# A chunked recurrence and two MoE stages: full-height closing products, an order that knows TensorE's columns, decay products on GpSimd, and an inverse that starts from two transposes

## The chip, the cores and the metric

The kernel runs on one core of a Trainium2 chip. The metric is the device time of one execution in microseconds (us). Before the change three runs took 1219.82, 1231.59 and 1233.6 us, a median of 1231.59. The trace comes from a further execution of 1221.59 us, whose span is 1219.8 us and whose mean granted TensorE clock is 0.944 of full speed.

Engines have short names in the rows: PE is TensorE's matmul and PEld its weight load, DVE is VectorE, ACT is ScalarE, POOL is GpSimd, and SP is the engine whose queue issues most DMAs.

## The reference

```python
# recurrence, for each of B*H = 4*8 heads, S = 768 steps, D = 40
y[:, :, t] = einsum('bhd,bhde->bhe', r_t, state)
Sa = einsum('bhde,bhe->bhd', state, a_t)
state = state * w_t[:, :, None, :] - einsum('bhd,bhe->bhde', Sa, b_t) \
        + einsum('bhd,bhe->bhde', v_t, k_t)
# first MoE, on x = y as 3072 tokens x 320 (d_ff 1024)
x = ((x @ w1) * (x @ w2)) @ w3 @ w_out
# second MoE (d_ff 2048)
h = x @ w_in
out = (h * cos(h)) @ w_out2
```

## The kernel before, in words

**The recurrence** is cut into 24 chunks of 32 steps (`C`, `NC`). The 32 heads are 16 pairs; in a pair one head has partitions 0 to 39 and the other 64 to 103 (`OD`, `EV`). For each chunk `prep` (L516) runs two scans of the decay, multiplies `a` by the decay `Dt` for each parity (the two products called GA, 40x512 on VectorE), and sends GA by DMA into a ring of 7 slots (`NB`; rows name the slots r_67 to r_79). `gstage` (L546) multiplies the scaled keys by GA on TensorE, and ScalarE copies the results into `lam`, a stack of 32x32 triangular matrices, and into the ring; GpSimd masks a triangle there.

Four chunks (`GC`) form a group. Their 512 triangular matrices are inverted together: `tinv_start` (L575) transposes `lam` into `Lt` in 32 pieces of 128x32 on VectorE, `tinv` (L591) solves diagonal blocks, the middle and the corner (matrices 0 to 11 of each partition on VectorE, 12 to 15 on GpSimd, side by side), and `tfin` (L660) transposes the result in one 128x1024 step into `TT`, from which TensorE reads. `lam`, `Lt`, the work tile and `TT` exist once, so the inverse of a group starts only when the one before is read out. Then each chunk goes through `mv`, `st_z`, `st_q`, `st_u`, `st_y`, `st_s`: small products on TensorE with copies by ScalarE, masks on X by GpSimd, and products on VectorE that write the next state. `st_y` (L739) has 16 products for each half of the pairs; its results for one parity lie in columns 64 to 103 of TensorE's array, for the other in 0 to 39. The output goes to DRAM (`yd`).

**The MoE stages.** After every two chunks a slab of 256 tokens is complete. `split_x` (L866) splits it into a rounded part `xh` and a remainder; `ab` (L874) computes a piece of `x @ w1` and `x @ w2` by sums of eight products of 128x256, the eighth of which has only 64 rows (`R[H0]` times `xr`). Products of the two are stored (`pd`). Beside it w3 and w_out are folded into one matrix, and weights are converted from 64-bit floats on VectorE (`conv`: three instructions a piece, tiles `f`, `w`, `r`). When the last slab is done the second phase runs, with the second MoE, which the change leaves as it is.

**What sets the order.** Nothing is issued while the functions above run: each call is recorded (`Program`, `Queue`), `link` finds what depends on what, and `emit` (L256) plans the order with a table of costs: an instruction starts when its engine is free and its inputs are there by the table, and of several that could start the one with the longest planned path to the end goes first (`far`). Instructions are then issued in the order of their planned starts, all from line 318, so every row says L318. On the chip each engine takes its instructions in that order, and a DMA queue too; an instruction that waits holds up those behind it.

Of the kernel before, what the change touches and what calls it, by code (L numbers as in the profile page):

```python
# [4 lines left out]

# [21 lines left out]
T2 = 256  # L27
# [102 lines left out]
class Program:  # L130

    STEP, DEEP = {True: 1.67, False: 0.457}, {True: 180, False: 185}
    COST = {
        ("scalar", "copy"): (205, 0.72), ("scalar", "activation"): (200, 0.9), ("vector", "tensor_tensor"): (155, 1.1),
        ("vector", "tensor_scalar"): (80, 1.3), ("vector", "scalar_tensor_tensor"): (80, 1.6),
        ("vector", "tensor_tensor_scan"): (80, 2.3), ("vector", "transpose"): (35, 1.8),
        ("vector", "tensor_reduce"): (147, 1.04), ("vector", "memset"): (60, 0.83),
        ("gpsimd", "tensor_tensor"): (330, 2.05), ("gpsimd", "affine_select"): (250, 1.2), ("gpsimd", "memset"): (110, 0.82),  # L140
    }
# [114 lines left out]
    def emit(self, tc, nc):  # L256
        self.link()
        N = len(self.calls)
        eng = [c[0] for c in self.calls]
        cost = [self.length(n) for n in range(N)]  # L260
        after = [[] for _ in range(N)]
        for n, d in enumerate(self.deps):
            for j in d:
                after[j].append(n)
        far = [0.0] * N
        hop = lambda n, m: self.HOP[eng[n]] if eng[m] != eng[n] else self.OWN[eng[n]]
        for n in reversed(range(N)):
            x = cost[n][1] + (self.ISSUE + self.BEGIN + self.END if eng[n] == "sync" else 0)
            far[n] = x + max([far[m] + hop(n, m) for m in after[n]], default=0)
# [6 lines left out]
        lanes, moved = deque([0.0] * self.LANES), 0.0  # L276
        for n in range(N):
            if not left[n]:
                heapq.heappush(later[eng[n]], (0.0, n))
        for k in range(N):  # L280
# [4 lines left out]
            n = heapq.heappop(ready[e])[1]  # L285
            if e == "tensor":
                if more is not None and not left[more] and self.mode(n) != mode and when[more] <= t + self.WAIT:
                    if n != more:
                        heapq.heappush(ready[e], (-far[n], n))
                        n = more  # L290
                        ready[e].remove((-far[n], n)) if (-far[n], n) in ready[e] else later[e].remove((when[n], n))
                        heapq.heapify(ready[e])
                        heapq.heapify(later[e])
                        t = max(t, when[n])
                more = self.sums.get(n)
            step, whole = cost[n]
            _, method, args, kw = self.calls[n]
            if method == "matmul":
                if self.mode(n) != mode:
                    t += self.SWITCH  # L300
                mode = self.mode(n)
            if method == "dma_start":
                t = max(t, lanes.popleft())
                moved = max(moved, t + step + self.BEGIN) + whole
                whole = moved + self.END + self.STORE * (kw["out"].space == DRAM) - t
                lanes.append(t + whole)
                step += self.GAP
            start[n] = (t, k)
            free[e], end = t + step, t + whole
            for m in after[n]:  # L310
                when[m] = max(when[m], end + hop(n, m))
                left[m] -= 1
                if not left[m]:
                    heapq.heappush(later[eng[m]], (when[m], m))
        with tc.manual_schedule():
            for n in sorted(range(N), key=lambda n: start[n]):
                e, method, args, kw = self.calls[n]
                getattr(getattr(nc, e), method)(*args, **kw)  # L318


class Kernel:
# [194 lines left out]
    def prep(self, c, alt=0):  # L516
# [70 lines left out]
    def quads(t, row, col, *dims):  # L587
# [277 lines left out]

    def split_x(self, xf):  # L866
        nc = self.nc
        xh, xl, xr = self.xh, self.xl, self.xr
# [3 lines left out]
        return xh, xl, xr  # L872

    def ab(self, s, x, f):  # L874

        nc = self.nc
        xh, xl, xr = x
# [134 lines left out]
    def weights_a(self):  # L1012

        self.ks = [self.fixed[t] for t in ("k1", "k2")]
        self.xf = self.place("mid", 128, 3, T2)
        t = lambda p, *f: self.place("xs", p, *f, dt=F32R)
        self.xh, self.xl, self.xr = t(128, 3, T2), t(128, 2, T2), t(64, T2)
        self.turns["p"] = deque(self.place("mid", 128, T2) for _ in range(PB))

    def turn(self, tag):  # L1020
# [305 lines left out]
```

## Time and profile before

| what | value |
|---|---|
| median of three runs | 1231.59 us (1219.82 to 1233.6) |
| profiled execution | 1221.59 us, span 1219.8 us |
| TensorE matmul (PE) busy | 1052.4 us, 86% of the span, 13536 instructions |
| VectorE (DVE) busy | 842.2 us, 69%, 1776 instructions |
| ScalarE (ACT) busy | 679.3 us, 56%, 1750 instructions |
| GpSimd (POOL) busy | 600.4 us, 49%, 734 instructions |

These shares are averages over stages with different limits. The span begins with an opening of 52.5 us; then six times an inverse of a group alternates with a stretch of chunks without one, until the last chunks and slabs end near 703 us; then comes a passage into the second phase, which starts near 808 us and lasts to the end. In the first 148 us the granted TensorE clock is low (0.67 to 0.69 from 52.5 on), later 0.89 to 1.00.

### The profile page before, as it was taken

The numbers are of one execution on the slowest core, as the hardware profiler recorded it, in microseconds if no ns is written. First come the engines' busy times: TensorE is split into PE (matmuls) and PEld (weight loads), VectorE is DVE, ScalarE is ACT, GpSimd is POOL, SyncE is SP. The second block draws the span as 40 slices with busy tenths as digits, with TensorE's granted clock in tenths as the row PEclk, the third lists the DMA queues.
The fourth block names the chain that finished last, engine by engine and source line by source line (L and its number), as shares of the span: only waits on it lengthen the run. The fifth ranks groups of instructions, "written<-read, shape, count | busy, mean of one in ns | idle before, by whom it ended". The sixth has DMA issues, their size and how long they took to land. (4 is left out here: it accounts for less than half of the span.)

```text
span 1219.8 us, 34120 instructions
## 1 busy us (share of the span) xinstructions
PE 1052.4 (86%) x13536; PEld 956.4 (78%) x13536; DVE 842.2 (69%) x1776; ACT 679.3 (56%) x1750; POOL 600.4 (49%) x734
## 2 busy tenths in 40 slices
PE   2434798869987998999889977999999999999997
PEld 1324687768776877878778865899999999999997
DVE  9797779668968887896796674785455554545444
ACT  5865545754676578478545542455455544555443
POOL 8666336435444533563566673463455443454222
PEclk9975799889988999999899987999999999999999
DMA  6643544443454445444446553411101111011000
GB/s 177 185 117 93 140 119 123 126 137 115 129 157 131 114 141 158 127 134 114 137 136 209 150 169 106 124 39 47 46 12 46 44 38 46 22 37 46 9 4 23
DMA packets 142128, 122.73 MB, mean 101 GB/s; under 512 B 68240, under 2 KB 114832, under 8 KB 140432
## 3 DMA queue, kind: packets, MB, share of 16 engines
q1 hardware_dynamic: 141824, 120.50, 34.4%
q8 instruction: 106, 1.74, 0.6%
q14 instruction: 54, 0.44, 0.1%
q10 hardware_dynamic: 144, 0.06, 0.0%
HBM read 86.95 MB, written 29.62 MB: 96 GB/s over the span
## 5 line engine op out<-in xcount | busy, mean ns | idle before, releaser
L318 PE MATMUL bank<-xs,w 128*128 128x256 f32 (+1 forms) x1536 | 281.3, 316 | 29.9 <-ACT xs L318 22.0
L318 PEld LDWEIGHTS bank<-xs,w 128*128 128x128 f32 (+1 forms) x1536 | 221.3, 200 | 75.2 <-ACT xs L318 23.8
L318 POOL TENSOR_TENSOR w<-w,w 128x512 fp32r<-128x512 f32 x96 | 127.9, 1333 | 237.5 <-ACT w L318 147.4
L318 POOL TENSOR_SCALAR_AFFINE_SELECT X<-X 32x256 f32<-32x256 f32 (+1 forms) x144 | 98.6, 685 | 113.2 <-ACT X L318 92.1
L318 ACT COPY mid<-bank 128x256 f32<-128x256 f32 (+2 forms) x190 | 71.7, 394 | 144.9 <-PE bank L318 138.3
L318 ACT COPY X<-bank 32x128 f32<-32x128 f32 (+1 forms) x384 | 124.3, 324 | 41.8 <-PE bank L318 36.3
L318 DVE SCALAR_TENSOR_TENSOR w<-w,bank 128x512 f32<-128x512 int32 x96 | 65.8, 687 | 117.6 <-ACT w L318 106.0
L318 ACT COPY r<-bank 64x160 f32<-64x160 f32 (+2 forms) x408 | 113.4, 281 | 43.7 <-PE bank L318 38.7
L318 PE MATMUL bank<-X,r 104*40 104x72 f32 (+3 forms) x3072 | 124.2, 238 | 12.8 <-POOL X L318 7.1
L318 DVE TENSOR_TENSOR X<-bank,mid 40x128 f32<-40x128 f32 (+1 forms) x276 | 97.9, 355 | 51.0 <-PE bank L318 46.0
L318 PE MATMUL bank<-xs,r 128*128 128x256 f32 x576 | 130.5, 282 | 0.5 <-DVE xs L318 0.5
L318 PE MATMUL bank<-D,r 128*128 128x256 f32 x576 | 129.2, 282 | 1.8 <-DVE w L318 1.7
L318 PEld LDWEIGHTS bank<-X,r 104*40 104x40 f32 (+3 forms) x3072 | 104.5, 118 | 25.1 <-POOL X L318 8.6
L318 ACT CAST w<-w 128x512 fp32r<-128x512 f32 x120 | 73.6, 620 | 85.5 <-PE bank L318 70.5
L318 PE MATMUL bank<-mid 32*32 32x72 f32 (+2 forms) x3040 | 92.6, 233 | 26.6 <-ACT r L318 18.6
L318 PE MATMUL bank<-r,w 128*128 128x320 f32 x432 | 107.7, 311 | 0.6 <-ACT r L318 0.6
L318 PEld LDWEIGHTS bank<-mid 32*32 32x32 f32 (+2 forms) x3040 | 72.2, 126 | 42.7 <-ACT r L318 20.3
L318 PEld LDWEIGHTS bank<-D,r 128*128 128x128 f32 x576 | 99.2, 189 | 2.5 <-DVE w L318 2.2
L318 PEld LDWEIGHTS bank<-xs,r 128*128 128x128 f32 x576 | 99.9, 189 | 0.7 <-DVE xs L318 0.7
L318 DVE TENSOR_TENSOR sh<-sh,sh 128x110 f32<-128x110 f32 (+6 forms) x216 | 85.1, 394 | 2.4
L318 DVE SCALAR_TENSOR_TENSOR w<-w 128x512 f32<-128x512 int32 x96 | 84.6, 882 | 1.9
L318 PE MATMUL bank<-more,w 128*128 128x320 f32 x360 | 84.9, 310 | 0.0
(92 smaller groups left out, 2278.9 us busy)
## 6 DMA issues: line engine op xcount, KB each, us to landing
pd<-mid SPq DMA_DIRECT2D x96, 128.0 KB
f<-w3t SPq DMA_DIRECT2D x32, 256.0 KB
sh<-kb SPq DMA_DIRECT2D x48, 160.0 KB
sh<-wa SPq DMA_DIRECT2D x96, 80.0 KB
X<-pd SPq DMA_DIRECT2D x6, 1024.0 KB
w<-pd SPq DMA_DIRECT2D x6, 1024.0 KB
w34d<-f SPq DMA_DIRECT2D x32, 160.0 KB
r<-wo SPq DMA_DIRECT2D x16, 320.0 KB
```

Of the source, the lines that this page charges most:

```text
L318: getattr(getattr(nc, e), method)(*args, **kw)
```

## The change

The eighth product of each sum in `ab` becomes a full 128-row one: the remainder `xl` has all three parts of x, and `xr` is gone. `split_x` needs one subtraction of 128x768 for it instead of two. The two GA products of each `prep` go from VectorE to GpSimd. `tinv_start` transposes `lam` in two instructions of sixteen 128x32 pieces each. In `emit`, the costs change; a matmul is planned as holding those of four 32-column quarters of the array that its result needs (`columns`, `array`), a change of kind (up to 32 rows, up to 64 rows, more; and the number type) waits until all quarters are free, and `beside` takes a ready product of the same kind whose quarters are free ahead of one whose quarters are not. `RUNS` is 0, so the random variations are not used. The plan being another, every engine's order changes.

```diff
@@ costs @@
-    STEP, DEEP = {True: 1.67, False: 0.457}, {True: 180, False: 185}
+    STEP, DEEP = {True: 1.67, False: 0.457}, 185
-        ... ("vector", "tensor_tensor"): (155, 1.1),
+        ... ("vector", "tensor_tensor"): (165, 1.25),
-        ("gpsimd", "tensor_tensor"): (330, 2.05), ...
+        ("gpsimd", "tensor_tensor"): (380, 2.3), ...
-    HOP = {"tensor": 95, "scalar": 65, "vector": 70, "gpsimd": 40, "sync": 60}
-    ISSUE, GAP, BEGIN, RATE, END, STORE, LANES, SWITCH, WAIT = 350, 55, 1350, 380, 1100, 600, 8, 120, 100
+    HOP = {"tensor": 140, "scalar": 110, "vector": 120, "gpsimd": 90, "sync": 60}
+    ISSUE, GAP, BEGIN, RATE, END, STORE, LANES, SWITCH, WAIT = 370, 60, 1350, 380, 1600, 600, 8, 90, 100
+    RUNS, LATE, VARY = 0, 500, {"vector": (0.9, 1.25), "gpsimd": (0.9, 1.4), "scalar": (0.95, 1.1)}
@@ length @@
-            a = kw["rhs"]
-            w = min(x for x in (32, 64, 128) if x >= size(kw["lhsT"]))
-            step = 4 + self.STEP[a.dtype == F32] * size(a) * w / 128
-            return step, self.DEEP[a.dtype == F32] + step * 128 / w / 2 if a.dtype == F32 else self.DEEP[False] + step
+            f = kw["rhs"].dtype == F32
+            step = 2 + self.STEP[f] * size(kw["rhs"])
+            return step, self.DEEP + step / (2 if f else 1)
@@ mode, columns, beside @@
-        return kw["lhsT"].ap[0][1] <= 32, kw["rhs"].dtype
+        return kw["lhsT"].ap[0][1] <= 32, kw["lhsT"].ap[0][1] <= 64, kw["rhs"].dtype
+    def columns(self, n):
+        out = self.aps[n][0][0]
+        r = out.offset // math.prod(out.tensor.shape[1:])
+        return range(r // 32, (r + out.ap[0][1] + 31) // 32)
+    def beside(self, n, t, mode, array, ready, far):
+        if self.kinds[n] == mode and max(array[i] for i in self.quarters[n]) > t + 20:
+            x = min((x for x in ready if self.kinds[x[1]] == mode and max(array[i] for i in self.quarters[x[1]]) <= t + 5), default=None)
+            if x:
+                ready.remove(x)
+                ready.append((-far[n], n))
+                heapq.heapify(ready)
+                return x[1]
+        return n
@@ run (was in emit) @@
-                if self.mode(n) != mode:
-                    t += self.SWITCH
+                else:
+                    n = self.beside(n, t, mode, array, ready[e], far)
+                ...
+                if self.kinds[n] != mode:
+                    t = max(t, *array) + self.SWITCH
+                mode = self.kinds[n]
+                t = max(t, *(array[i] for i in self.quarters[n]))
+                for i in self.quarters[n]:
+                    array[i] = t + step
+                step = max(13, min(array) - t)
@@ prep @@
-            v.tensor_tensor(out=GA[R, par, :, 0:C], in0=self.a[R], in1=Dt[R], op=ALU.mult)
+            nc.gpsimd.tensor_tensor(out=GA[R, par, :, 0:C], in0=self.a[R], in1=Dt[R], op=ALU.mult)
@@ tinv_start @@
-        for t in range(C):
-            v.transpose(out=self.Lt[:, (C // 2 - 1 - t) % C, :], in_=self.lam[:, t, :])
-            if t % 4 == 3:
-                yield
+        h = C // 2
+        for t in range(0, C, h):
+            v.transpose(out=self.Lt[:, t:t + h][:, ::-1], in_=self.lam[:, t:t + h])
+            yield
@@ split_x @@
-        nc.gpsimd.tensor_tensor(out=xl, in0=xf[:, 0:2], in1=xh[:, 0:2].bitcast(F32), op=ALU.subtract)
-        nc.gpsimd.tensor_tensor(out=xr, in0=xf[H0, 2], in1=xh[H0, 2].bitcast(F32), op=ALU.subtract)
+        nc.gpsimd.tensor_tensor(out=xl, in0=xf, in1=xh.bitcast(F32), op=ALU.subtract)
@@ ab @@
-            ops += [(R[:, w, fs], xh[:, 2])] + [(T[i][0][:, w, fs], xl[:, i]) for i in range(2)] + [(R[H0, w, fs], xr)]
+            ops += [(T[i][0][:, w, fs], xl[:, i]) for i in range(2)] + [(R[:, w, fs], xh[:, 2]), (R[:, w, fs], xl[:, 2])]
```

VectorE's order where the first inverse begins, before. `D` is the decay scan's result, `sh_63` and `sh_65` hold `lam`, GA and the inverse's tiles, `f_92` is a piece of weights being converted; the third row is a GA product, the fourth the start of `tinv_start`:

```order
L318 SCALAR_TENSOR_TENSOR D<-sh_63,sh_65 104x512
L318 TENSOR_SCALAR f_92<-f_92 128x256
L318 TENSOR_TENSOR sh_63<-sh_63,D 40x16x32
L318 STREAM_TRANSPOSE sh_65<-sh_63 128x32 x30
L318 SCALAR_TENSOR_TENSOR f_92<-f_92 128x256
L318 TENSOR_TENSOR sh_65<-sh_65,sh_63 128x2x15
```

The same place in the order after the change:

```order
L357 SCALAR_TENSOR_TENSOR D<-sh_63,sh_65 104x512
L357 TENSOR_SCALAR f_92<-f_92 128x256
L357 STREAM_TRANSPOSE sh_65<-sh_63 128x16x32 x2
L357 SCALAR_TENSOR_TENSOR f_92<-f_92 128x256
L357 TENSOR_TENSOR sh_65<-sh_65,sh_63 128x2x15
```

The GA product has left the queue, and two transposes stand for the many.

GpSimd's order in the second inverse, before. `sh_63` and `sh_65` rows are its share of the inverse, `f_94` a weight's remainder:

```order
L318 TENSOR_TENSOR sh_63<-sh_65 128x2x8
L318 TENSOR_TENSOR sh_65<-sh_63 128x16x16
L318 TENSOR_TENSOR f_94<-f_92,f_94 128x256
L318 TENSOR_TENSOR sh_65<-sh_65 128x16x8
L318 TENSOR_TENSOR sh_65<-sh_65 128x16x4
L318 TENSOR_TENSOR sh_65<-sh_65 128x16x2
L318 TENSOR_TENSOR sh_63<-sh_65 128x2x8
```

The corresponding steps after the change (`r_69` is a slot of the ring that is masked, `xs<-mid,xs` the split of a slab):

```order
L357 TENSOR_TENSOR sh_63<-sh_65 128x2x8
L357 TENSOR_TENSOR sh_65<-sh_63 128x16x16
L357 TENSOR_TENSOR sh_63<-sh_63,D 40x16x32 x2
L357 TENSOR_TENSOR f_94<-f_92,f_94 128x256
L357 TENSOR_TENSOR sh_65<-sh_65 128x16x8
L357 AFFINE_SELECT r_69<-r_69 32x512
L357 TENSOR_TENSOR sh_65<-sh_65 128x16x4
L357 TENSOR_TENSOR f_94<-f_92,f_94 128x256
L357 TENSOR_TENSOR xs<-mid,xs 128x768
L357 TENSOR_TENSOR sh_65<-sh_65 128x16x2
L357 AFFINE_SELECT r_69<-r_69 32x512
L357 TENSOR_TENSOR sh_63<-sh_65 128x2x8
```

The pair of GA products now stands between two steps of the inverse, with masks of the ring and the split of a slab among the steps behind it.

## Rows read from the trace of the kernel before

**Rows 1.** Windows view: stretch, length, busy us (instructions) by engine, clock, DMA, GB/s.
```profile
core 0: us, PE busy (x) PEld busy (x) DVE busy (x) ACT busy (x) POOL busy (x), PEclk, DMA share, GB/s
...
147.80:211.10 63.30, 60.30 (x904) 50.33 (x903) 54.41 (x156) 32.13 (x97) 33.40 (x53) 0.96 0.46 126
211.10:263.00 51.90, 41.69 (x792) 35.69 (x792) 31.32 (x67) 37.13 (x116) 18.91 (x25) 0.90 0.45 128
...
485.80:547.50 61.70, 56.68 (x910) 47.72 (x900) 56.72 (x156) 36.72 (x113) 35.66 (x57) 0.94 0.46 132
547.50:576.30 28.80, 27.53 (x521) 23.65 (x521) 18.61 (x39) 23.86 (x75) 9.67 (x14) 1.00 0.43 115
...
626.50:703.00 76.50, 72.92 (x1390) 61.63 (x1393) 53.21 (x118) 37.72 (x105) 46.66 (x62) 1.00 0.63 185
703.00:808.40 105.40, 83.99 (x625) 74.74 (x617) 72.83 (x108) 42.59 (x93) 56.26 (x57) 0.89 0.39 122
808.40:1219.80 411.40, 404.51 (x3145) 403.93 (x3145) 206.66 (x299) 204.98 (x369) 172.99 (x127) 1.00 0.11 32
```

**Rows 2.** Timeline of VectorE at ends of inverses: start us, us, what.
```profile
107.97 1.99 DVE L318 STREAM_TRANSPOSE mid<-sh 128x1024 f32<-128x1024 f32 x1 [0.94 <-POOL sh L318]
...
210.29 0.53 DVE L318 TENSOR_REDUCE sh<-sh 128x24 f32<-128x384 f32 x1
...
211.07 2.01 DVE L318 STREAM_TRANSPOSE mid<-sh 128x1024 f32<-128x1024 f32 x1
```

**Rows 3.** Timeline of TensorE around closing products, narrow windows, 427 to 648 us.
```profile
427.23 1.35 PE L318 MATMUL bank<-xs,w 128*128 128x256 f32 x10
...
645.28 0.28 PE L318 MATMUL bank<-xs,w 128*128 128x256 f32 x1
645.49 0.29 PE L318 MATMUL bank<-mid 32*32 32x72 f32 x4
...
646.72 0.28 PE L318 MATMUL bank<-xs,w 128*128 128x256 f32 x1
...
646.93 0.38 PE L318 MATMUL bank<-xs,w 64*128 64x256 f32 x1
...
647.24 0.38 PE L318 MATMUL bank<-xs,w 128*128 128x256 f32 x1
...
647.46 0.40 PE L318 MATMUL bank<-xs,w 128*128 128x256 f32 x2
```

**Rows 4.** Timeline of TensorE, two runs of y products.
```profile
167.67 1.86 PE L318 MATMUL bank<-X,r 104*40 104x72 f32 x64
...
454.46 1.19 PE L318 MATMUL bank<-X,r 104*40 104x72 f32 x16
```

**Rows 5.** Groups by form: operation, shapes, count, busy us, mean ns, idle before.
```profile
L318 POOL TENSOR_TENSOR w<-w,w 128x512 fp32r<-128x512 f32 x96 | 127.9, 1333 | 237.5 <-ACT w L318 147.4 <-PE bank L318 85.8 <-DVE w L318 4.3
...
L318 DVE TENSOR_TENSOR sh<-sh,D 40x512 f32<-40x512 f32 x44 | 37.9, 862 | 10.8 <-PE bank L318 10.1
...
L318 DVE STREAM_TRANSPOSE sh<-sh 128x32 f32<-128x32 f32 x192 | 20.5, 169 | 0.3 <-ACT sh L318 0.2
...
L318 POOL TENSOR_TENSOR xs<-mid,xs 128x512 fp32r<-128x512 f32 x12 | 18.4, 1532 | 7.3 <-ACT xs L318 6.8 <-DMA r<-win 0.5
...
L318 POOL TENSOR_TENSOR xs<-mid,xs 64x256 fp32r<-64x256 f32 x12 | 12.0, 1003 | 0.0
L318 DVE STREAM_TRANSPOSE mid<-sh 128x1024 f32<-128x1024 f32 x6 | 12.0, 2004 | 1.4 <-POOL sh L318 1.3
...
L318 DVE TENSOR_TENSOR X<-sh,D 40x512 f32<-40x512 f32 x4 | 2.7, 682 | 0.1
```

**Rows 6.** Windows view of GpSimd in the first inverse.
```profile
55.50:108.00 52.50, 34.53 (x50) 0.67 0.43 119
```

**Rows 7.** Tile f: duration in ns min/median/max, first and last start, forms.
```profile
L318 DVE TENSOR_SCALAR f<-f x72: 190/287/2511, 6.1 to 591.0; 128x256 int32<-128x256 int32 x56, 128x160 int32<-128x160 int32 x16
```

**Rows 8.** The chain of waits behind 703 us: start us, us, what.
```profile
714.05 7.29 DMA r<-win
```

**Rows 9.** Waits: engine, line, waited for: us in total, times, longest us.
```profile
POOL X L318 <- ACT X L318: 96.5, 60, 8.5
```

More of the change, by code (lines that the diff above doesn't have):

```diff
@@ L2 @@
 import math
+import random
 from collections import deque
@@ L130 @@
 class Program:
-    STEP, DEEP = {True: 1.67, False: 0.457}, {True: 180, False: 185}
+    STEP, DEEP = {True: 1.67, False: 0.457}, 185
     COST = {
-        ("scalar", "copy"): (205, 0.72), ("scalar", "activation"): (200, 0.9), ("vector", "tensor_tensor"): (155, 1.1),
+        ("scalar", "copy"): (205, 0.72), ("scalar", "activation"): (200, 0.9), ("vector", "tensor_tensor"): (165, 1.25),
         ("vector", "tensor_scalar"): (80, 1.3), ("vector", "scalar_tensor_tensor"): (80, 1.6),
@@ L139 @@
         ("vector", "tensor_reduce"): (147, 1.04), ("vector", "memset"): (60, 0.83),
[L140 removed]
+        ("gpsimd", "tensor_tensor"): (380, 2.3), ("gpsimd", "affine_select"): (250, 1.2), ("gpsimd", "memset"): (110, 0.82),
     }
     OWN = {"vector": 34, "scalar": 12, "gpsimd": 78, "tensor": -150, "sync": 60}
[L143 to L144 removed]
+    HOP = {"tensor": 140, "scalar": 110, "vector": 120, "gpsimd": 90, "sync": 60}
+    ISSUE, GAP, BEGIN, RATE, END, STORE, LANES, SWITCH, WAIT = 370, 60, 1350, 380, 1600, 600, 8, 90, 100
+    RUNS, LATE, VARY = 0, 500, {"vector": (0.9, 1.25), "gpsimd": (0.9, 1.4), "scalar": (0.95, 1.1)}
     def __init__(self):
@@ L253, in mode, with run @@
         kw = self.calls[n][3]
-        return kw["lhsT"].ap[0][1] <= 32, kw["rhs"].dtype
-    def emit(self, tc, nc):
-        self.link()
-        N = len(self.calls)
[L259 to L265, printed above, removed]
+        return kw["lhsT"].ap[0][1] <= 32, kw["lhsT"].ap[0][1] <= 64, kw["rhs"].dtype
[12 more added lines that the diff above has]
+        return n
+    def run(self, far, cost, after, rng):
+        N = len(self.calls)
+        eng = self.eng
         hop = lambda n, m: self.HOP[eng[n]] if eng[m] != eng[n] else self.OWN[eng[n]]
-        for n in reversed(range(N)):
-            x = cost[n][1] + (self.ISSUE + self.BEGIN + self.END if eng[n] == "sync" else 0)
-            far[n] = x + max([far[m] + hop(n, m) for m in after[n]], default=0)
         left = [len(d) for d in self.deps]
@@ L275, in emit @@
         mode = more = None
-        lanes, moved = deque([0.0] * self.LANES), 0.0
+        lanes, moved, array = deque([0.0] * self.LANES), 0.0, [0.0] * 4
         for n in range(N):
@@ L279, in emit @@
                 heapq.heappush(later[eng[n]], (0.0, n))
-        for k in range(N):
+        for _ in range(N):
             t, e = min((max(free[e], 0.0 if ready[e] else later[e][0][0]), e) for e in engines if ready[e] or later[e])
@@ L285, in emit @@
             n = heapq.heappop(ready[e])[1]
+            step, whole = cost[n]
             if e == "tensor":
[L287 to L294, printed above, removed]
@@ L295, in emit @@
-                more = self.sums.get(n)
-            step, whole = cost[n]
-            _, method, args, kw = self.calls[n]
-            if method == "matmul":
-                if self.mode(n) != mode:
-                    t += self.SWITCH
-                mode = self.mode(n)
-            if method == "dma_start":
+                if more is not None and more != n and not left[more] and self.kinds[n] != mode and when[more] <= t + self.WAIT:
+                    heapq.heappush(ready[e], (-far[n], n))
+                    n = more
+                    x = (-far[n], n)
+                    (ready if x in ready[e] else later)[e].remove(x if x in ready[e] else (when[n], n))
+                    heapq.heapify(ready[e])
+                    heapq.heapify(later[e])
+                    t = max(t, when[n])
+                    step, whole = cost[n]
+                else:
+                    n = self.beside(n, t, mode, array, ready[e], far)
+                    step, whole = cost[n]
@@ L303, in emit @@
+                more = self.sums.get(n)
+                if self.kinds[n] != mode:
[5 more added lines that the diff above has]
+                step = max(13, min(array) - t)
+            elif e == "sync":
                 t = max(t, lanes.popleft())
                 moved = max(moved, t + step + self.BEGIN) + whole
-                whole = moved + self.END + self.STORE * (kw["out"].space == DRAM) - t
+                whole = moved + self.END + self.STORE * (self.calls[n][3]["out"].space == DRAM) - t
+                if rng:
+                    whole += rng.expovariate(1 / self.LATE)
@@ L306, in emit @@
                 lanes.append(t + whole)
                 step += self.GAP
-            start[n] = (t, k)
+            elif rng:
+                step = whole = whole * rng.uniform(*self.VARY[e])
+            start[n] = t
             free[e], end = t + step, t + whole
@@ L314, in emit, with sorted @@
                     heapq.heappush(later[eng[m]], (when[m], m))
+        return start
+    def emit(self, tc, nc):
+        self.link()
+        N = len(self.calls)
+        eng = self.eng = [c[0] for c in self.calls]
+        cost = [self.length(n) for n in range(N)]
+        pe = [n for n in range(N) if eng[n] == "tensor"]
+        self.kinds, self.quarters = {n: self.mode(n) for n in pe}, {n: self.columns(n) for n in pe}
+        after = [[] for _ in range(N)]
+        for n, d in enumerate(self.deps):
+            for j in d:
+                after[j].append(n)
+        far = [0.0] * N
+        for n in reversed(range(N)):
+            x = cost[n][1] + (self.ISSUE + self.BEGIN + self.END if eng[n] == "sync" else 0)
+            far[n] = x + max([far[m] + (self.HOP[eng[n]] if eng[m] != eng[n] else self.OWN[eng[n]]) for m in after[n]], default=0)
+        runs = [self.run(far, cost, after, random.Random(k)) for k in range(self.RUNS)]
+        mean = self.run([-sum(x) for x in zip(*runs)] if runs else far, cost, after, None)
         with tc.manual_schedule():
-            for n in sorted(range(N), key=lambda n: start[n]):
+            for n in self.sorted(mean, after):
                 e, method, args, kw = self.calls[n]
                 getattr(getattr(nc, e), method)(*args, **kw)
+    def sorted(self, mean, after):
+        left = [len(d) for d in self.deps]
+        heap = [(mean[n], n) for n in range(len(left)) if not left[n]]
+        heapq.heapify(heap)
+        while heap:
+            _, n = heapq.heappop(heap)
+            yield n
+            for m in after[n]:
+                left[m] -= 1
+                if not left[m]:
+                    heapq.heappush(heap, (mean[m], m))
 class Kernel:
@@ L867, in split_x @@
         nc = self.nc
-        xh, xl, xr = self.xh, self.xl, self.xr
+        xh, xl = self.xh, self.xl
         nc.scalar.copy(xh, xf)
-        nc.gpsimd.tensor_tensor(out=xl, in0=xf[:, 0:2], in1=xh[:, 0:2].bitcast(F32), op=ALU.subtract)
-        nc.gpsimd.tensor_tensor(out=xr, in0=xf[H0, 2], in1=xh[H0, 2].bitcast(F32), op=ALU.subtract)
-        return xh, xl, xr
+        nc.gpsimd.tensor_tensor(out=xl, in0=xf, in1=xh.bitcast(F32), op=ALU.subtract)
+        return xh, xl
     def ab(self, s, x, f):
         nc = self.nc
-        xh, xl, xr = x
+        xh, xl = x
         T, R = self.w12(f // 2)
@@ L1016, in weights_a @@
         t = lambda p, *f: self.place("xs", p, *f, dt=F32R)
-        self.xh, self.xl, self.xr = t(128, 3, T2), t(128, 2, T2), t(64, T2)
+        self.xh, self.xl = t(128, 3, T2), t(128, 3, T2)
         self.turns["p"] = deque(self.place("mid", 128, T2) for _ in range(PB))
```

## The prediction

> **What bounds the kernel now.** I read the windows view first, cut where the inverse of each group of four chunks begins (its first 128x32 transpose) and ends (the 128x1024 transpose of `tfin`). Three kinds of stage come out [rows 1]. In the second to fifth inverse stages VectorE is the limit: 54.41 of 63.30 us busy in the first of them, 56.72 of 61.70 in the last, and its timeline shows `tfin` starting 0.78 us after the inverse's last reduction began [rows 2]: nothing else was awaited. In the stages between (the first and the last are shown) VectorE is only 60 and 65% busy and TensorE 80 and 96%; there the chunk recurrence and the MoE products beside it go through TensorE. From 626.50 to 703.00 TensorE is busy 72.92 of 76.50 us. From 703.00 to 808.40 DMAs and weight conversions decide. From 808.40 on TensorE is busy 404.51 of 411.40 us with products that the change leaves as they are, so 411 us are fixed. The loop that repeats is: `tfin` of a group, its recurrence, a slot of the ring free, prep and gstage, the copies into `lam`, transposes, inverse, the next `tfin`; `tfin` to `tfin` takes 103.1 us the first time (108.0 to 211.1 [rows 2]).
>
> The sum is made against the profiled execution, 1221.59 us (span 1219.8). It stands 10.0 under the median of the runs, 1231.59, and 1.8 over the fastest, 1219.82.
>
> **The closing products.** In the stretch at 646.72 the steps from start to start are 0.21 (128 rows to the 64-row closer), 0.31 (closer to the next 128-row product) and 0.22 (to the one behind) [rows 3]. Ten 128-row products in a row take 1.35 us from 427.23, a step of (1.35-0.28)/9 = 0.119. So a lone closer between 128-row products costs 0.74 - 3 x 0.119 = 0.38. Where a narrow product follows, the 128-row product itself pays a step of 0.21 (645.28 to 645.49), the closer's way is 0.21 + 0.31: (0.52 - 0.21 - 0.119) = 0.19 is saved. In the program's order the 192 closers form 170 stretches, 57 followed by a 128-row product, 113 by a narrow one: 57 x 0.38 + 113 x 0.19 = 43 us of TensorE. By stretches 92 lie in the five inverse stages from the second on (23 us), 30 in the stages between (8), 26 in 626.5 to 703 (7), 22 behind it (6).
>
> **The order by columns.** The y products are 768, each two records in the trace and 40 columns wide, in the upper half of the array for one parity and the lower for the other. Sixteen records of one column half take 1.19 us, 0.074 each; sixty-four with halves alternating take 1.86, 0.029 each [rows 4]. I take 0.04 for the difference, since the short row's length holds one full latency. Neighbours of the same half fall from 235 to 84 in the new order: 151 x 2 x 0.04 = 12 us, nearly all in the stages between. Against it stand more changes between column modes (56 to 95, at about 0.1 us: 4 us). Changes of tile mode of any kind fall from 845 to 624; beyond the closers I give this nothing.
>
> **VectorE's relief.** The 48 GA products leave VectorE (862 ns mean for 44 of them), and 192 transposes become 12 [rows 5]. The 192 are busy 20.5 us in all, 0.107 each (they overlap, so the mean of one, 169 ns, is longer); the sixteenfold form has half the elements of the 128x1024 transpose (2004 ns), so 1.0 us. Per group 32 x 0.107 - 2 x 1.0 = 1.4 us. Between the first transpose and `tfin` I count every VectorE instruction in both orders at its row's mean: 298 us before and 277 after over the five stages from the second on. Of the 21 us, 7 are transposes, 9 are the ten GA products that stood there, and 5 are conversions that the new order sets in the stages between, where VectorE has room.
>
> **What GpSimd takes on.** No trace has a 40x512 product there. Below, it costs no less than on VectorE undisturbed (about 0.68, the X form's mean of 682); above, no more than the 128x512 subtract with a mean of 1532 [rows 5]. I take 1.36, near the 1333 of the 96 128x512 products. The twelve splits go from 1532 + 1003 ns to one of 128x768; by elements 1.5 x 1.33 = 2.0 us, 0.5 saved, between 0.2 and 0.7. Outside the first inverse GpSimd is busy about half of these stages, so 2.7 us for a pair is covered. In the first inverse it is not obvious: from 55.50 to 108.00 GpSimd is busy 34.53 us of 52.50 [rows 6] and gets six GA products and several memsets more; by row lengths about 52 to 54. VectorE's work there is 58 us by row means in both orders, so I give this stage 0 (at worst +5).
>
> Two copies of GA into the ring and the next load of `wa` stand behind each pair in SP's queue, in order; a pair that ends 1 to 2 us later holds them and what is behind them as long. A chunk comes every 26 us of the 103, so I cost this at nothing; without that cover it would be 24 x 0.7 = 16 us at most.
>
> What the engine choice costs beyond its own length is contention. A 128x256 or 128x160 TENSOR_SCALAR on VectorE lasts 287 ns at the median and 2511 at the longest [rows 7], so instructions here do stretch one another. The Trainium skill speaks against the move: GPSIMD Engine Reference, section 4.1 (Engine selection), keeps two-input elementwise work on VectorE because GpSimd is about twice as slow, and its Key points say the two engines share their SBUF interfaces. The factor agrees with the rows (1.36 taken against 0.68); if each pair held VectorE for its whole 2.7 us, five stages would give back 13 us and the sum would be about 1200. Of such stretching I take 3 us over the five stages.
>
> **The passage behind 703.** Its chain is made of conversions and weight loads: one wait of 7.29 us for `r<-win` stands in it [rows 8]. The 6 us of TensorE saved there are covered by those. After the last write of `yd` two more of the weight loads remain than before (19 for 17) on SP's queue: +3 us, between 0 and +14, the two longest such waits. The start: GA leaves VectorE while GpSimd has memsets; -1, between -4 and +3.
>
> **Sum.** Inverse stages -21 + 3 = -18 (VectorE decides, TensorE's 23 fall there but buy little by themselves). Stages between: 8 + 12 - 4 = 16 of TensorE at three quarters, since 80 to 96% of them is TensorE's: -12. The tail, TensorE-bound: -7. Passage +3, start -1. Together -35: 1221.6 - 35 = 1186.6. I say **1187**.
>
> **The rivals.**
> Rival one, slower: GpSimd holds up the recurrence. Its share of the inverse and the selects on X now queue behind the GA pair, and GA itself waits for VectorE's scan. GpSimd has waited up to 8.5 us for one ScalarE copy of X [rows 9]; a GA pair stuck ahead of the X select by the same amount adds 8.5 + 2.7 = 11 us per group. On five groups +56 with the inverse's gain lost: 1221.6 - 17 + 56 = 1260. It decides from (35/5) = 7 us a group; below 3.6 only the inverse's gain goes. For it: the pair stands between steps of the inverse in the new order, with selects of the ring behind. Against it: GpSimd idles 26 to 30 us in each such stage, and the scan comes early. Chance 0.06.
> Rival two: the loop closes elsewhere. The relief of VectorE is filled with other work or contention, and TensorE in the stages between waits for ScalarE's copies as before: only the tail, half of the stages between and a few us stay, -7 -6 -2 = -15: 1207. For it: from 211.10 to 263.00 TensorE idles a fifth and VectorE two fifths at once, so something else closes the loop there, and nothing in the change is aimed at that. Chance 0.22.
> Rival three: everything lands. TensorE's 23 us in the inverse stages (its clock 0.94 to 0.96 there, busy up to 95%) also come home, as the products beside the inverse stop holding up the recurrence: 43 + 12 - 4 + 21 = 72, less 3: 1153. Against it: TensorE and VectorE overlap in the same stages, so their savings need not add. Chance 0.15.
> Rival four, the change does not do what it says to TensorE: the steps of 0.21, 0.31 and 0.22 come from the end of an accumulation and not from 64 rows, and 128-row closers keep them. Then only VectorE's 18 and part of the y products remain: 1221.6 - 18 - 6 + 3 = 1201. Against it: the 0.21 stands ahead of the closer, where no sum has ended, and a 128-row product ahead of a narrow one shows the same 0.21. Chance 0.04.
>
> **Numbers.** The forecast of 1187 has 0.53, its own range 1172 to 1200 from the bounds above. Range of all: 1152 to 1215, which takes in rival three and four and most of two; left out are rival one and edges, some 0.15. A measurement of this kernel tells about 1% (12.3 us) from no change, so faster means under 1219.3: the forecast, rivals three and four, and four fifths of two, 0.53 + 0.15 + 0.04 + 0.18 = 0.90, of which I keep 0.86 since the runs of before alone differ by 14; within 1%: 0.08; slower by more: 0.06.
>
> **What would show it.** Stages from first transpose to `tfin` 4 us shorter each in the middle four; no 64-row product of `bank<-xs,w`, and 128-row runs with steps of 0.12 throughout; y products near 0.03 a record; GA on GpSimd near 1.36; the last stage after 808.40 unchanged at 411. Wrong would be: `tfin` no longer right behind the last VectorE reduction but behind GpSimd, X selects that start late, or conversions on VectorE longer than before.

## The result, and the profile after

The changed kernel takes 1187.94 us (median of four runs, 1185.24 to 1191.89); beside it the kernel before took 1225.75 (1219.82 to 1233.6). The ratio is 0.969, 95% interval 0.9611 to 0.9769. The profiled execution has a span of 1183.4 us against 1219.8. The forecast was 1187; but the time did not come from where the forecast had put it, as the stages show.

I cut both traces at the same events: first transpose of each inverse, `tfin`, the last chunk's output (the last `D<-bank,D`), the end of the last closing sum of `ab`, the first product `bank<-xs,r` of the second phase. Lengths in us; "kept" means that the instructions stand in the order of the kernel named, engine by engine. Each column is one execution, and a stage varies from one to the next: a second trace of the changed kernel (run 11) has 301.0 for inverses two to six, 169.7 for the stages between them and 81.0 for the tail. Run 8's column is of an execution of 1207.95 us, 8 under its median.

| stage | before | changed | 1: closers, old order kept | 2: GA on GpSimd, old order kept | 4: changed, short closers | 6: changed, GA on VectorE | 8: new order, old work |
|---|---|---|---|---|---|---|---|
| to the first inverse | 52.5 | 52.4 | 52.7 | 56.9 | 51.9 | 49.4 | 49.1 |
| first inverse | 55.4 | 68.3 | 55.5 | 62.7 | 68.2 | 62.0 | 58.0 |
| chunks before the second | 39.8 | 25.9 | 39.8 | 37.1 | 26.7 | 29.6 | 33.1 |
| inverses two to six | 300.7 | 295.7 | 297.5 | 315.2 | 314.3 | 311.8 | 330.3 |
| the stages between these | 178.0 | 168.2 | 172.2 | 180.4 | 175.6 | 150.3 | 148.8 |
| last `tfin` to last chunk | 85.2 | 81.1 | 80.9 | 86.1 | 86.5 | 78.8 | 88.4 |
| to the last `ab` product | 47.3 | 35.1 | 35.9 | 44.4 | 38.8 | 34.7 | 41.4 |
| to the second phase | 45.8 | 41.5 | 46.6 | 46.0 | 39.0 | 41.0 | 43.1 |

The windows of the changed kernel answer to [rows 1]; the second inverse and the stage behind it, the fifth and the stage behind it, the tail, the passage, the second phase, and ahead of them the first inverse:

```profile
52.40:120.60 68.20, 21.41 (x240) 17.71 (x240) 65.51 (x119) 43.86 (x137) 59.85 (x74) 0.50 0.48 129
...
146.50:206.30 59.80, 52.65 (x788) 44.92 (x782) 50.04 (x108) 28.03 (x82) 32.10 (x50) 0.91 0.41 114
206.30:254.80 48.50, 41.90 (x845) 36.36 (x848) 32.85 (x69) 39.19 (x122) 23.83 (x32) 1.00 0.52 146
...
474.20:539.30 65.10, 54.20 (x970) 48.41 (x971) 56.16 (x124) 39.92 (x122) 46.48 (x63) 0.92 0.49 137
539.30:563.60 24.30, 22.17 (x462) 19.28 (x462) 14.03 (x31) 19.90 (x63) 8.81 (x13) 0.93 0.35 88
...
610.50:687.00 76.50, 71.23 (x1509) 64.37 (x1505) 53.42 (x122) 41.74 (x116) 46.90 (x61) 0.97 0.65 187
687.00:772.00 85.00, 67.20 (x524) 64.88 (x523) 60.55 (x98) 38.13 (x83) 55.66 (x54) 0.92 0.46 144
772.00:1183.40 411.40, 404.51 (x3142) 403.94 (x3141) 218.94 (x306) 207.75 (x370) 177.61 (x129) 1.00 0.11 33
```

In the first inverse GpSimd (the last of the five busy times, 59.85 of 68.20 us) is now nearly full; in the second VectorE has lost 4.4 us of work and the stage only 3.5; the fifth has become longer. From its first product the second phase takes 415.0 us before and 415.2 now.

The groups by form answer to [rows 5]:

```profile
L357 PE MATMUL bank<-xs,w 128*128 128x256 f32 x1536 | 230.0, 299 | 25.4 <-ACT xs L357 14.9 <-DVE mid L357 9.4 <-POOL xs L357 0.7
L357 POOL TENSOR_TENSOR sh<-sh,D 40x512 f32<-40x512 f32 x44 | 63.1, 1435 | 20.6 <-PE bank L357 15.0 <-issue 3.0 <-DMA mid<-rd 0.5
L357 POOL TENSOR_TENSOR xs<-mid,xs 128x768 fp32r<-128x768 f32 x12 | 23.7, 1973 | 5.1 <-ACT xs L357 4.6 <-DMA sh<-wa 0.3 <-POOL X L357 0.2
...
L357 DVE STREAM_TRANSPOSE sh<-sh 128x512 f32<-128x512 f32 x12 | 8.0, 693 | 0.9 <-ACT sh L357 0.9
```

The products of `ab` are busy 230.0 us, 51 less than the page of before has for the same 1536; with the order kept (run 1, second line) they are busy 241.2, 40 less:

```profile
L318 PE MATMUL bank<-xs,w 128*128 128x256 f32 (+1 forms) x1536 | 281.3, 316 | 29.9 <-ACT xs L318 22.0
L318 PE MATMUL bank<-xs,w 128*128 128x256 f32 x1536 | 241.2, 302 | 31.4 <-ACT xs L318 23.1 <-DVE mid L318 7.9 <-POOL xs L318 0.2
```

GA takes 1.44 us on GpSimd (1.36 forecast), the split 1.97 (2.0), a big transpose 0.69 (1.0).

**Behind the last chunk.** These windows are of the kernel before, first the whole stretch from the last chunk to the last `ab` product, then a part of it (stretch, length, busy us and instructions of PE, PEld, DVE, ACT, POOL, granted clock):

```profile
711.70:758.70 47.00, 34.15 (x168) 27.83 (x168) 26.18 (x37) 11.82 (x29) 22.99 (x25) 0.78 0.46 146
736.60:745.00 8.40, 8.34 (x30) 6.99 (x31) 2.23 (x5) 0.57 (x2) 2.09 (x3) 0.50 0.28 90
```

And of the changed kernel, the same stretch and two parts:

```profile
691.50:726.40 34.90, 21.31 (x148) 20.17 (x148) 24.82 (x41) 11.35 (x27) 24.67 (x26) 0.85 0.58 177
705.30:711.80 6.50, 6.46 (x32) 6.13 (x32) 5.49 (x5) 0.84 (x3) 6.43 (x7) 0.60 0.34 98
712.60:716.70 4.10, 4.09 (x32) 3.89 (x32) 3.54 (x5) 0.89 (x3) 3.69 (x4) 1.00 0.47 132
```

TensorE is busy 12.8 us less, the stretch is 12.1 us shorter. The changed kernel has 20 products fewer in it (148 instead of 168), so run 1, which has the same 168, is the cleaner comparison. Here are its whole stretch and its share of 64 products, and then the same 64 of the kernel before:

```profile
698.60:734.60 36.00, 24.07 (x168) 22.82 (x168) 23.30 (x37) 11.60 (x28) 23.18 (x25) 0.86 0.58 182
721.00:730.00 9.00, 8.30 (x64) 7.83 (x64) 6.37 (x13) 2.15 (x7) 4.69 (x7) 1.00 0.41 128
736.66:753.25 16.59, 16.41 (x64) 13.04 (x64) 6.53 (x13) 2.21 (x7) 3.79 (x5) 0.61 0.23 76
```

The long closers alone make the stretch 11.4 us shorter (table), and TensorE's idle time in it stays at 12 to 14 us, so the DMAs and conversions did not cover what TensorE saved. Not all of it is the closers' own: the 64 products take 8.1 us less, of which the eight closers among them are some 4 us by the two prices below (five at the lower clock, three at the full one), and the rest goes with the granted clock, 0.61 there before and 1.00 in run 1. Whether the short closers brought the clock down is not shown; in run 2, which has them too, it was 0.85 in the stretch.

In the slice at 736.60 the granted clock is 0.50, the lower level, after an idle of 4.82 us ahead of 736.66. There a closer costs more than [rows 3] gave. TensorE's timeline of before in that slice:

```profile
738.97 0.63 PE L318 MATMUL bank<-xs,w 128*128 128x256 f32 x2
...
739.52 0.58 PE L318 MATMUL bank<-xs,w 64*128 64x256 f32 x1
...
740.03 0.58 PE L318 MATMUL bank<-xs,w 128*128 128x256 f32 x1
...
740.41 0.63 PE L318 MATMUL bank<-xs,w 128*128 128x256 f32 x2
```

Four steps from 738.97 to 740.41 take 1.44 us. Without a closer a step is 0.21 there (a pair lasts 0.63, of which one is 0.42), so four would be 0.84: the closer costs 0.60 us, against 0.38 at the full clock.

**The first inverse.** GpSimd's timeline of the changed kernel ahead of `tfin` (start us, us), and two rows of VectorE, its last reduction of the inverse and `tfin`:

```profile
116.70 1.26 POOL L357 TENSOR_TENSOR sh<-sh 128x64 f32<-128x64 f32 x1
117.92 0.91 POOL L357 TENSOR_TENSOR w<-f,w 128x256 fp32r<-128x256 f32 x1
118.79 1.83 POOL L357 TENSOR_TENSOR sh<-sh 128x32 f32<-128x32 f32 x2
```
```profile
113.21 0.55 DVE L357 TENSOR_REDUCE sh<-sh 128x24 f32<-128x384 f32 x1
...
120.65 1.91 DVE L357 STREAM_TRANSPOSE mid<-sh 128x1024 f32<-128x1024 f32 x1 [0.43 <-POOL sh L357]
```

VectorE's own share ended at 113.8, GpSimd's at 120.6, and `tfin` waited for it. (In [rows 2] the reduction of the second inverse ends 0.25 us ahead of its `tfin`.)

### The profile page after: what moved, and what is told of

Its sections match the earlier page's. It is cut to its first block, busy times and chain, and to the rows that moved or that the text cites. A ratio compares the mean times of both kernels' runs of the same rounds, so it can differ in the third digit from the quotient of the medians.

```text
span 1183.4 us, 33942 instructions
## 1 busy us (share of the span) xinstructions
PE 1002.5 (85%) x13536; PEld 932.0 (79%) x13536; DVE 823.4 (70%) x1548; ACT 680.1 (57%) x1750; POOL 671.9 (57%) x770
## 4 chain that ended last, share of the span: by engine, by line
PE 41%; DVE 4%; DMA 2%; issue 1%; ACT 1%; POOL 1%; SPq 0%; ACTq 0%; POOLq 0%
PE bank L357 41%; DVE r L357 2%; DVE w L357 1%; DMA X<-pd 1%; DMA pd<-mid 1%; DVE sh L357 1%; DVE X L357 1%; DVE mid L357 0%; ACT X L357 0%; ACT mid L357 0%; DMA r<-win 0%; POOL w L357 0%; ACT w L357 0%; POOL xs L357 0%; ACT xs L357 0%
## 5 line engine op out<-in xcount | busy, mean ns | idle before, releaser
L357 PE MATMUL bank<-xs,w 128*128 128x256 f32 x1536 | 230.0, 299 | 25.4 <-ACT xs L357 14.9
L357 PEld LDWEIGHTS bank<-xs,w 128*128 128x128 f32 x1536 | 202.0, 198 | 42.1 <-ACT xs L357 16.0
L357 ACT COPY X<-bank 32x288 f32<-32x288 f32 (+1 forms) x384 | 124.6, 325 | 39.5 <-PE bank L357 33.8
L357 PE MATMUL bank<-X,r 128*40 128x72 f32 (+3 forms) x3072 | 125.3, 240 | 25.3 <-POOL X L357 20.3
L357 PEld LDWEIGHTS bank<-X,r 128*40 128x40 f32 (+3 forms) x3072 | 102.2, 120 | 43.0 <-POOL X L357 23.5
L357 ACT CAST w<-w 128x512 fp32r<-128x512 f32 x120 | 72.9, 620 | 83.1 <-PE bank L357 62.7
L357 PE MATMUL bank<-r,w 128*128 128x320 f32 x432 | 104.3, 310 | 0.0
L357 PE MATMUL bank<-sh 104*64 104x144 f32 x576 | 59.5, 323 | 41.7 <-POOL sh L357 26.0
L357 DVE TENSOR_TENSOR w<-bank,w 128x512 f32<-128x512 f32 x96 | 66.0, 688 | 39.9 <-ACT w L357 39.9
L357 ACT ACTIVATE w<-bank 128x512 int32<-128x512 f32 x96 | 57.2, 597 | 62.5 <-PE bank L357 62.4
```

## The experiments

The reading of the two traces gave this theory: the closing products carry most of the gain, because TensorE is on the path in more places than the forecast had; the move of GA to GpSimd costs time, and the new order makes up for it. The rivals: the new order carries the gain, or VectorE's relief does. Runs 1, 2, 3, 4, 5 and 9 keep an order, so that one part changes alone; for that the planner plans as before, and the instruction is replaced when it is issued:

```diff
-                e, method, args, kw = self.calls[n]
-                getattr(getattr(nc, e), method)(*args, **kw)
+                for e, method, args, kw in self.swap.get(n, [self.calls[n]]):
+                    getattr(getattr(nc, e), method)(*args, **kw)
```

**Run 1, the closers alone.** The remainder `xr` gets 128 rows:

```diff
+ swap: nc.tensor.matmul(P[:, w], lhsT=R[:, w, fs], rhs=xr, start=False, stop=True)
+ swap: nc.gpsimd.tensor_tensor(out=xr, in0=xf[:, 2], in1=xh[:, 2].bitcast(F32), op=ALU.subtract)
```

> The kernel before with its order on every engine kept, instruction by instruction; only the 192 closing products of 64 rows read 128 rows. Theory (the 64-row step costs TensorE time that lies on the chain above all behind the last inverse, 12 us of it behind the last chunk where the clock is at its lower level): about 1195, that is 23 to 30 us less than the kernel before, with 10 to 16 us of it behind the last chunk. Rival (the gain of the change comes from the new order, and the closers are hidden beside VectorE and DMAs): 1212 or more. Rival (the steps come from the end of a sum and not from the rows): no change, 1222.

Measured: 1197.14 us (1190.91 to 1198.99), ratio 0.9725 (0.9649 to 0.98), the kernel before 1227.6 beside it. The closers alone are worth 30 us, at the upper end. Both rivals fall. The two traces differ by 23.6 us, since the traced execution of before lies 6 under that median. By the table 15 of these come from behind the last `tfin`, 11.4 of them between last chunk and last `ab` product, and 9 from the loop: 3.2 from inverses two to six and 5.8 from the stages between.

**Run 2, GA on GpSimd alone.**

```diff
- swap: v.tensor_tensor(out=GA[R, par, :, 0:C], ...)
+ swap: nc.gpsimd.tensor_tensor(out=GA[R, par, :, 0:C], ...)
```

> The kernel before with its order kept, only the 48 decay products (GA) issued by GpSimd at their places in the order. Theory (VectorE's relief in the inverse is taken back by GpSimd, whose share of the inverse becomes the last one, most of all in the first): between 1218 and 1230, with the first inverse longer by 3 to 10 us and the later ones shorter by 1 or 2 each. Rival (VectorE alone bounds the inverse, as the prediction had it): 9 us less, about 1212.

Measured: 1247.52 us (1243.55 to 1251.66), ratio 1.0143 (1.0065 to 1.0222). It is slower, by more than expected, and the first inverse is longer by 7.3. The waits of this run over its first 120 us, and behind them those of the kernel before over its first 111 (engine, what it waited for, us in total, times, longest us):

```profile
PE bank L318 <- POOL sh L318: 66.2, 5, 22.7
```
```profile
PE bank L318 <- DVE sh L318: 34.4, 3, 19.7
PE bank L318 <- issue: 14.6, 1, 14.6
```

The five waits of 66.2 us are TensorE's ahead of products of `gstage`. Ahead of the same products it waits 53.0 us in the kernel before: 34.4 for VectorE, 14.6 where the trace names no releaser, and 4.0 for ScalarE. So `gstage` waits 13 us longer. From the end of the scan that makes `Dt` to the end of the second GA product it is 373 us in this run against 328, summed over 24 chunks: 1.9 more per chunk, of which 1.0 is the longer pair itself (2 x (1.36 - 0.85)) and the rest waiting ahead of it. The second inverse starts 8.9 us later.

Inverses two to six are 14.5 longer in this trace, but 8.7 of it lie in the fifth, where the granted clock was 0.81 (0.94 before), and run 3 does not repeat it. The total does not hang on the clock: an execution of run 2 at 0.935 took 1243.55 us, one of before at 0.937 took 1227.6.

VectorE gets less relief than the move should give. GA was busy 37.9 + 2.7 us there [rows 5], but the busy time of VectorE falls only from 842.2 to 825.1 us. Its other instructions, the same ones in the same order, are 21 us longer in sum (894.2 against 873.3); without the move that sum changes by 0.6 (run 1). Back on VectorE in the new order (run 5) it falls by 28 (882.8 to 855.0). So VectorE's instructions are stretched while GpSimd has the products, and half of the relief goes that way.

**Run 3, all three parts in the old order.** Runs 1, 2 and 9 together.

> All three parts of the change in the kernel's work (128-row closers, GA on GpSimd, two transposes for 32), issued in the order of the kernel before. Theory (the parts carry most of the gain, the order the rest): about 1192, so that the new order is worth some 5 us. Rival (the new order carries it): 1205 or more.

Measured: 1211.11 us (1208.26 to 1215.71), ratio 0.9855 (0.9764 to 0.9947). The theory's number is missed; the rival's holds. The reason is run 2: GA takes back half of the closers' 30. The first 160 us show where: these are the windows up to the second inverse of this run, of run 1 and of run 9.

```profile
0.00:159.90 159.90, 58.48 (x913) 50.47 (x913) 118.61 (x219) 95.98 (x279) 112.52 (x144) 0.67 0.47 132
0.00:148.00 148.00, 60.90 (x914) 52.94 (x914) 126.88 (x264) 95.40 (x279) 91.29 (x127) 0.80 0.50 142
0.00:147.00 147.00, 60.41 (x937) 51.62 (x937) 124.04 (x236) 95.78 (x279) 89.37 (x128) 0.66 0.52 143
```

This run differs from run 1 by GA and the transposes. Its second inverse starts 11.9 us later, and its whole span is 11.9 us longer (1208.1 and 1196.2); inverses two to six take 299.6 us against 297.5. So here the move costs its time in the opening and the first inverse, and next to nothing in the loop. The low clock did not make it: run 9 has 0.66 there and is not late.

From here to the changed kernel are some 20 us (0.9855 and 0.969), and these the new order gives. That is more than run 8 shows for the order alone, and a part of it may be better places for GA, but the intervals of runs 3 and 8 are too wide to show it.

**Run 4, short closers in the new order.** The swap of run 1 the other way round, `R[H0, w, fs]` with `xl[H0, 2]`.

> The changed kernel with its order kept, only the 192 closing products read 64 rows again. Theory: the reverse of the first run, and more, since this order does not bundle the closers: 1215 to 1240, with most of the loss behind the last inverse and in the stages between inverses. Rival (the order carries the gain, closers are hidden): under 1200.

Measured: 1217.21 us (1213.9 to 1220.09), ratio 0.9896 (0.9822 to 0.997): 29 us over the changed kernel by the medians, 25 by the ratios. The place is another than expected: 18.6 of them are in inverses two to six (13.3 against the trace of run 11), 7.4 in the stages between, 5.4 in the tail. VectorE's waits from the second inverse to the last `tfin` show why. `mid` is the tile where ScalarE puts one sum of `ab`, for VectorE to multiply it with the other; `X` belongs to the chunk. First the kernel before, then run 9, the changed kernel and this run:

```profile
DVE X L318 <- PE bank L318: 29.2, 25, 4.7
DVE mid L318 <- ACT mid L318: 20.3, 23, 2.9
```
```profile
DVE X L318 <- PE bank L318: 32.8, 25, 4.7
DVE mid L318 <- ACT mid L318: 27.1, 28, 3.3
```
```profile
DVE X L357 <- PE bank L357: 34.7, 32, 5.9
DVE mid L357 <- ACT mid L357: 30.2, 25, 7.1
```
```profile
DVE mid L357 <- ACT mid L357: 52.1, 39, 7.6
DVE X L357 <- PE bank L357: 42.1, 34, 7.0
```

With short closers VectorE waits 21.9 us more for ScalarE's copies of `ab` sums and 7.4 more for TensorE's products on X. Both stand among the inverse's steps in its queue, so a sum that TensorE finishes late stops the inverse behind it. TensorE is in fact the busier engine there: 281.2 of 314.3 us in this run's inverses two to six, VectorE 250.9.

**Run 5, GA back on VectorE, the new order kept.** The swap of run 2 the other way round.

> The changed kernel with its order kept, the 48 decay products (GA) issued by VectorE at their places in that order. Theory (in the first inverse GpSimd ends last because of the pairs; later VectorE has some idle time): the first inverse 5 to 10 us shorter, the second to sixth 0 to 2 us longer each, the time between 1180 and 1195. Rival (the prediction's: VectorE bounds the inverse, and GA there costs 9 us and more): 1197 or more.

Measured: 1194.29 us (1185.51 to 1196.63), ratio 0.971 (0.9627 to 0.9793), not to be told from the changed kernel's 0.969. The first inverse stays at 67.9, so the pairs alone do not make its length, and that part of the theory falls. `tfin` still waits for GpSimd there: GpSimd's share ends at 116.59 and `tfin` starts at 116.62, though GpSimd is busy only 54.0 us of the 67.9. That its order does it is argued, not shown.

**Run 6, GA on VectorE, planned anew.** One word of the source: `v` for `nc.gpsimd` in `prep`.

> The changed kernel with GA on VectorE and the order planned anew for it, the other parts of the change kept. Theory (the move alone cost 20 us in the old order, and the new order only makes up for it): 1170 to 1184, below the changed kernel. Rival (the move pays once the order knows of it): 1192 or more.

Measured: 1178.74 us (1174.88 to 1180.42), ratio 0.9592 (0.9522 to 0.9662). As the theory had it, this beats the changed kernel; run 12 repeats it.

**Run 7, a mixture.** `(v if c < 8 else nc.gpsimd)` in `prep`.

> The changed kernel with GA of the first eight chunks on VectorE, of the other sixteen on GpSimd, planned anew. Theory: the opening and the first inverse as with VectorE (first inverse under 60 us), the later stages as in the changed kernel, 1172 to 1184. Rival (what the first inverse loses is made up before the second one starts, as in the changed kernel, whose second inverse starts at 146.5 against 147.8): 1188, no difference.

Measured: 1182.01 us (1180.21 to 1186.68), ratio 0.9636 (0.9549 to 0.9722). Inside the expectation, though the first inverse is 62.0 and not under 60, and no better than run 6.

**Run 8, the new order alone.** The program of before under the changed planner.

> The work of the kernel before (64-row closers, GA on VectorE, 32 transposes), issued in an order that the new planner makes for it. Theory (the new order saves by columns and by timing some 10 us, closers apart): 1210 to 1220. Rival (the new order is good only for the moved GA): 1225 or more. Rival (it carries some 23 us, the distance of the third run to the changed kernel): 1205 or less.

Measured: 1215.84 us (1207.95 to 1223.67), ratio 0.9898 (0.9805 to 0.9992): 12 us by the ratio and 15 by the medians, as the theory had it, with a wide interval.

**Run 9, the transposes alone.** In the old order, the big transpose at the place of each sixteenth, the other fifteen left away.

> The kernel before with its order kept, only the 192 transposes of 128x32 replaced by 12 of 128x512 at the place of the last of each sixteen. The prediction's price: 1.4 us per group on a path of five to six groups, 7 us, about 1220. Rival (the sum of the first three runs: all three parts together took 12 us less than the closers' and GA's effects added up): 10 to 12 us less, 1214 to 1217. Rival (off the path): no change.

Measured: 1230.94 us (1222.81 to 1238.61), ratio 1.0018 (0.9977 to 1.0059). No change: the third expectation. The transposes are busy 8.0 us instead of 20.5, and nothing becomes shorter.

**Run 10, without the preference for free columns.** `n = self.beside(...)` is left out of run 6.

> The kernel of the sixth run (changed kernel, GA on VectorE) without the step that prefers a ready product whose columns are free; the rest of the planner as it is, planned anew. Theory (products of one column half in succession cost TensorE 0.04 us a record more): 5 to 12 us slower, 1184 to 1191, with y products in longer runs of one half. Rival (the gain of the new order is its costs and not the columns): 1176 to 1181.

Measured: 1176.54 us (1176.09 to 1179.9), ratio 0.9565 (0.9511 to 0.9619): the same as runs 6 and 12. Records of y products that follow one of the same half rise from 146 to 278 in the trace, at 68 ns instead of 33; these 5 us of TensorE are not on the path.

**Runs 11 and 12, the changed kernel and run 6 once more,** side by side on one chip.

> The changed kernel once more, beside the next: 1185 to 1190.

> The kernel of the sixth run once more, on the same chip as the changed kernel: if leaving GA on VectorE is the better choice, 7 to 12 us under it; if the ninth part of a hundred between them was the chip's, the same.

Measured: 1189.64 us (1187.34 to 1193.03), ratio 0.9668 (0.9624 to 0.9713), and 1180.96 us (1177.4 to 1186.56), ratio 0.9595 (0.9544 to 0.9646). No execution of the one reaches the other, and the clock does not explain it: run 12 took 1186.56 us at a granted clock of 0.913 and 1179.02 at 0.917, run 11 1189.38 at 0.930 and 1187.34 at 0.939. Leaving GA on VectorE is worth 8.7 us by the medians when each version has an order of its own; 5.5 of the 10.3 us between the first traces of the two lie ahead of the second inverse (141.0 us in run 6, 146.5 in the changed kernel), and run 6 is the best version found, with run 10 its equal.

## Why the prediction came out right, and which steps were wrong

The time was right because two errors cancelled, and that is luck. By the table inverses two to six gave 5.0 us (none in the trace of run 11) where the sum had 18, and the passage gave 16.5 where the sum had a loss of 3. The stages between gave 9.8 for 12, the tail 4.1 for 7.

- **The closers' price** was right: 43 us of TensorE worked out, 40 fewer busy with the order kept; that the 64 rows are the cause is shown by runs 1 and 4. **Where it counts was wrong.** The sum gave them 8 x 3/4 + 7 = 13 us on the path. They brought 30 (23.6 between the traces). "The 6 us of TensorE saved there are covered" failed: the long closers alone made the stretch behind the last chunk 11.4 us shorter, some 4 of it by the clock. The prediction's own window from 703.00 to 808.40 has TensorE busy 83.99 of 105.40 us [rows 1], so it was no bystander there. "TensorE's 23 fall there but buy little by themselves" held in the old order (3.2 us in run 1) and failed in the new one (18.6 in run 4). That is the mechanism of rival three, which I had given 0.15.
- **VectorE's relief** was the failed step: -18 in the inverse stages, because VectorE alone was held to bound them. The work did leave (inverses two to six: 254.7 us busy instead of 266.7), and it came back as waiting: from the second inverse to the last `tfin` VectorE waits 15.4 us more for `ab` sums and products on X than before, and 10.4 more in run 9, where the transposes alone bring nothing. High VectorE occupancy and a `tfin` right behind its last reduction had made it look like the sole limit; but [rows 1] have TensorE busier in the same stage, 60.30 of 63.30 us against 54.41. GA on GpSimd costs 20 us alone in the old order (run 2), 9 where each version has its own order (runs 11 and 12), and nothing that can be told with the new order held (run 5). It costs them ahead of the second inverse, where the chain begins with GA, and a product that takes 1.44 us instead of 0.85, behind GpSimd's other work, makes `gstage` later. Rival one had the engine right, not the place: TensorE's waits for masks on X are 11.8 us in run 2 and 11.5 before (20.3 in the changed kernel, but 21.7 in run 6 too, so that is the new order's). Of the stretching that the move brings I took 3 us over five stages; run 2 shows 21 over the whole execution.
- **What the Trainium skill says** against the move (GPSIMD Engine Reference, section 4.1) was the better guide. The trace agrees with its factor of about two (1435 ns against 862 on the busy VectorE of before, 1.7 times; 2.1 times the 682 of the X form). The agreement that the prediction claims was none, since its 1.36 was my own estimate. I had weighed it at 3 us.
- **The first inverse**, "0 (at worst +5)": +12.9, GpSimd last. Run 5 shows that the pairs alone do not make it. The time was made up before the second inverse, which starts 1.3 us earlier than before.
- **The columns**: neighbours of one half in the trace fell from 424 to 159 records, 35 ns each, 9 us for the 12 forecast. The stages between gave 9.8 us from the second on, of which the closers alone give 5.8 (run 1). That the columns gave the rest is not shown; run 10 speaks against it.
- **The passage**, +3 for two more loads: it became 16.5 us shorter. **The start**, -1: 0.1. **The second phase** was unchanged, as forecast.

What stays open: which of the planner's new costs makes the 12 to 15 us of run 8, and why the first inverse is so long in the order of the changed kernel with GA on either engine (68.3 and 67.9, against 62.0 where the order is made for VectorE).

## What to carry to other kernels

An engine that is 85 to 90% busy in a stage is not its sole limit when its queue holds work that waits for another: look first whether another engine is busier in the same window, and ask which instructions stand between the steps of the long chain in that queue, and who releases them. Before work is moved to a slower engine to relieve a busy one, follow the moved result itself: if the next stage's chain starts with it, its latency counts, most of all in the opening, where little else covers it, and the relief may not. Try each part in an order that is held, since a planner hides one part's loss in another's gain.

## What the runs showed of the hardware

A 128x512 transpose in 32x32 blocks took 693 ns where one of 128x1024 took 2004; the sixteen that it replaces were busy 1.7 us. A lone 64-row product among 128-row ones cost 0.38 us at a granted clock of 1.00 and 0.60 at 0.50, which I had not allowed for. With GA on GpSimd the other VectorE instructions took 894.2 us in sum, without it 873.3, in the same order.
